# The last expert's output is rounded earlier and subtracted later; one transposed output and a scaling of rows move, in a fused retention, mixture-of-experts and feed-forward kernel

## The chip, the cores and the metric

The kernel runs on one core of a Trainium2 chip. The metric is the time of one execution on the device in microseconds (us): the median of the runs. The profile comes from one execution of its own, whose span runs from its first to its last instruction.

## The reference

Three stages follow one another on 1536 tokens of 512 features. A retention layer of 8 heads makes the rows x. A mixture of 8 experts sends each row to the expert with the largest logit, and scales that expert's output by the row's gate weight. A feed-forward stage with 2048 hidden features applies a rational function between its two matrix products.

```python
state = gamma * state + einsum('bhd,bhe->bhde', k_t, v_t)
y_t = scale * einsum('bhd,bhde->bhe', q_t, state)
...
expert_idx = argmax(x @ w_gate, axis=1)          # 8 experts, at most capacity rows each
h = maximum(einsum('ecd,edf->ecf', disp, w1), 0) # 512 -> 1024
y = einsum('ecf,efd->ecd', h, w2)                # 1024 -> 512
out[i] = gate_w[i] * y[expert_idx[i], pos[i]]
...
h = x @ w_in                                     # 512 -> 2048
P = a[0] + a[1]*h + a[2]*h*h + a[3]*h*h*h
Q = 1 + |b[0]|*|h| + |b[1]|*h*h
return (P / (Q + 1e-6)) @ w_out                  # 2048 -> 512
```

## The kernel before

Each fp32 factor of a product is split in two: a high part (`yh`, `xh`, `whi`, `gh`), rounded to the type fp32r by ScalarE, and a low part (`yl`, `xl`, `wlo`, `gl`), the difference, made by VectorE or GpSimd. A product is three matmuls: high by high, low by high, high by low.

Every engine works through its instructions in the order in which the Python code issues them; nothing reorders them. A semaphore makes an instruction wait for what it needs from another engine, and everything behind it on its own engine waits too.

**Experts.** `moe` loops over experts 1 to 7 (expert 0 is done in `first_expert`). The first layer of an expert has four blocks, `fp` 0 to 3, of 24 matmuls of 224 columns each. Behind each block stand a ReLU on ScalarE (`h`), the low part on VectorE, the split of another half of a weight block (`prep_next`: `whi` on ScalarE, `wlo` on VectorE) and a slot for decoding weights of the feed-forward stage (`dec_slot`, tile `gq`). The second layer has four quarters, `q` 0 to 3, of eight pairs of matmuls, which add up in `acc`: two tiles of two PSUM banks each. Behind the last quarter `y_pair` rounds each tile to `yh` (L856) and subtracts to `yl` (L857, L859). Both go to columns that start at a register's value, which a TENSOR_LOAD reads on both engines (`start`).

**The rows of the next experts.** Rows of expert `e` are fetched by an indirect DMA on GpSimd's queue (`gather`, two pieces for each expert, four buffers `xg`), scaled by their gate weight on ScalarE (`x_gate`, L954, in place), transposed by TensorE into a PSUM bank (`expert_x`, L964) and split into `xh` and `xl` (L967, L968). The tag `xt` of this bank has one buffer, which is bank 0; `y_turn` uses it too, for the transposed output `ytp` of the rest of expert 0 (`y0`, 96 rows), which it then splits (L850, L856, L857).

**Feed-forward.** `ffn_step(n)` issues block n of 48: `ffn_a` (first layer, 12 matmuls of 512 columns into one of the four banks with the tag `fh`, which `ffn_e` of block n-4 must have read), `ffn_i`, `ffn_p`, `ffn_r` and `ffn_e` (the rational function, on ScalarE, VectorE and GpSimd), `ffn_g` (high and low part `gg`) and, five blocks behind, `ffn_b` (second layer, 12 matmuls into the four banks with the tag `fo`). Steps 0 to 3 are issued between the quarters of expert 7, step 4 behind the first tile's `y_pair`. Blocks 0 to 7 read rows 0 to 1023 of `yh` and `yl`, while the last expert writes at row 1312 or behind it. The banks of the tag `fo` are those of the two `acc` tiles: the pool `pf` is opened when `pn` has been closed.

```python
"fh": (0, 1, 2, 3), "fo": (4, 5, 6, 7)      # banks; "xt": (0,)
...
self.pn = self.pool("pn", space=PSUM, stack=st)   # acc, in moe
...
self.pf = self.pool("pf", space=PSUM, stack=st)   # fo, in ffn
```

Of the kernel before, what the change touches and what calls it, by code (L numbers as in the profile page):

```python
# [7 lines left out]
F32 = mybir.dt.float32  # L8
# [5 lines left out]
AF = mybir.ActivationFunctionType  # L14
ALU = mybir.AluOpType
# [6 lines left out]
E = 8  # L22
# [18 lines left out]
NA = 48  # L41
# [43 lines left out]
class Build:  # L85
# [766 lines left out]

    def y_put(self, ps, k, at, more=None):
        yh, yl = self.yh[:, k, at], self.yl[:, k, at]
        tt = self.nc.vector.tensor_tensor
        self.nc.scalar.activation(out=yh, in_=ps, func=AF.Copy)  # L856
        tt(out=yl if more is None else yl.bitcast(F32), in0=ps, in1=yh.bitcast(F32), op=ALU.subtract)  # L857
        if more is not None:
            tt(out=yl, in0=more, in1=yl.bitcast(F32), op=ALU.add)  # L859

# [111 lines left out]
    def moe(self):  # L972
        nc = self.nc
        with ExitStack() as st:
# [8 lines left out]
            for e in range(1, E):  # L983
                xh, xl = (t.pop(e)[:, :, 0:W] for t in (self.xh, self.xl))
                h = {}
                for fp in range(4):
                    i = 4 * e + fp // 2
# [15 lines left out]
                    self.prep_next()  # L1003
                    if fp < 3 and fp != 1 and e + 1 < E:
                        self.x_gate(e + 1, fp // 2)
                    if fp % 2 and e + 1 < E:
# [4 lines left out]
                    if (e, fp) == (1, 0):  # L1011
                        self.y_turn(self.y0, 1)
                acc = [self.wide(i, "acc").rearrange("p (o n) -> p o n", o=2)[:, :, 0 : 2 * W] for i in range(2)]
                acc = [t.rearrange("p o (a n) -> p o a n", a=2) for t in acc]
                for q in range(4):
# [14 lines left out]
                    if q == 3:  # L1030
                        at = bass.ds(self.start(e), W)
                        for i in range(2 if e < E - 1 else 0):
                            self.y_pair(acc, i, at)
                    self.dec_slot(8 * e + 4 + q)
                    if e == E - 1:
                        self.ffn_step(q)
                    if q % 2:
                        del self.whi[4 * e + 2 + q // 2], self.wlo[4 * e + 2 + q // 2]
            for i in range(2):
                self.y_pair(acc, i, at)  # L1040
                if i == 0:
                    self.ffn_step(4)

    def y_pair(self, acc, i, at):
        self.y_put(acc[i][:, :, 0], slice(2 * i, 2 * i + 2), at, acc[i][:, :, 1])

# [181 lines left out]
    def ffn(self):  # L1228
        with ExitStack() as st:
            self.fp = self.pool("ffn", stack=st)  # L1230
            self.pf = self.pool("pf", space=PSUM, stack=st)
            for n in range(5, NA):
                self.ffn_step(n)
            self.ffn_tail()
# [179 lines left out]
```

## Time and profile before

| | before |
|---|---|
| time, median of 3 runs | 514.39 us (513.76 to 514.82) |
| the profiled execution's own time | 512.93 us |
| its span | 511.2 us |
| TensorE busy | 496.5 us |
| VectorE busy | 413.9 us |
| ScalarE busy | 365.4 us |
| GpSimd busy | 243.5 us |

The profiled execution's own time is 1.73 us above its span, and the median of the runs lies another 1.46 us above that. In the profile PE is TensorE's matmuls, DVE is VectorE, ACT is ScalarE and POOL is GpSimd; a small q behind an engine's name is its sequencer. L and a number is a line of the kernel.

### The profile page before, as it was taken

Reading aid. Unit: us, or ns where it says so; the run is one execution under the profiler, and the core shown is the slowest. Engines: PE = TensorE matmul, PEld = TensorE weight load, DVE = VectorE, ACT = ScalarE, POOL = GpSimd, SP = SyncE. Lnnn points to the kernel's source line nnn. Section 1 sums busy time; section 2 is a strip of 40 time slices with the busy share of each in tenths; the row PEclk is TensorE's granted clock in tenths of the full one; section 3 lists DMA queues with packets and bytes.
Section 4 is the critical chain, followed back from the end, with each engine's and each line's share of the span. In section 5 each row is a group of like instructions: output and inputs, shape, how many; then the busy total and the mean of one; then the engine's idle time right before and its main releaser. Section 6 shows DMA issues by size and latency. Waiting matters only on the chain.

```text
span 511.2 us, 9195 instructions
## 1 busy us (share of the span) xinstructions
PE 496.5 (97%) x3401; PEld 430.9 (84%) x3401; DVE 413.9 (81%) x602; ACT 365.4 (71%) x605; POOL 243.5 (48%) x187
## 2 busy tenths in 40 slices
PE   8999999999999999999879999999999999999995
PEld 5888878999999999998668888888888888888883
DVE  2579858789997999894686989999899998865973
ACT  1356638868767677664857989989999987776760
POOL 2621041034243744543424547667568764354774
PEclk9999999999999999999989999999999999999999
DMA  8999676899987999971400002222013100000203
GB/s 304 408 414 388 215 226 205 325 324 297 320 298 225 382 306 269 322 243 30 164 0 2 0 4 79 83 82 83 27 58 113 52 1 0 2 1 0 83 21 144
DMA packets 27409, 83.07 MB, mean 163 GB/s; under 512 B 4960, under 2 KB 5216, under 8 KB 27360
## 3 DMA queue, kind: packets, MB, share of 16 engines
q1 hardware_dynamic: 24304, 73.52, 42.2%
q0 software_dynamic: 2624, 7.35, 4.1%
q10 hardware_dynamic: 432, 1.57, 1.0%
q8 instruction: 27, 0.44, 0.3%
q14 instruction: 22, 0.18, 0.1%
HBM read 71.94 MB, written 10.49 MB: 161 GB/s over the span
## 4 chain that ended last, share of the span: by engine, by line
PE 62%; DVE 3%; ACT 2%; POOL 1%; issue 1%; POOLq 0%; ACTq 0%; DVEq 0%
PE h L1116 8%; PE h L1117 8%; PE h L1118 8%; PE o L1187 8%; PE o L1188 8%; PE o L1189 8%; PE acc L373 7%; PE e L996 2%; PE e L995 2%; PE e L994 2%; POOL out L1218 1%; PE tp L964 1%; DVE fw L1153 1%; DVE h L1154 1%; ACT fx L1129 0%
## 5 line engine op out<-in xcount | busy, mean ns | idle before, releaser
L154 DVE TENSOR_TENSOR wlo<-raw,whi 128x1024 fp32r<-128x1024 f32 x80 | 112.5, 1418 | 12.8 <-ACT whi L149 12.3
L1167 POOL TENSOR_TENSOR gg<-fx,gg 128x512 fp32r<-128x512 f32 x47 | 61.0, 1299 | 76.1 <-issue 60.8
L149 ACT ACTIVATE whi<-raw 128x1024 fp32r<-128x1024 f32 x80 | 83.2, 1056 | 2.0 <-PE acc L373 1.3
L1187 PE MATMUL o<-whi,gg 128*128 128x512 f32 x192 | 75.5, 393 | 4.6 <-DVE yl L859 4.6
L1188 PE MATMUL o<-wlo,gg 128*128 128x512 f32 x192 | 75.2, 392 | 0.0
L1189 PE MATMUL o<-whi,gg 128*128 128x512 f32 x192 | 75.2, 392 | 0.0
L1116 PE MATMUL h<-yh,whi 128*128 128x512 f32 x192 | 74.8, 390 | 0.0
L1118 PE MATMUL h<-yh,wlo 128*128 128x512 f32 x192 | 74.8, 389 | 0.0
L1117 PE MATMUL h<-yl,whi 128*128 128x512 f32 x192 | 74.7, 389 | 0.0
L373 PE MATMUL acc<-h,whi 128*128 128x448 f32 x224 | 71.3, 377 | 0.0
L1142 POOL TENSOR_TENSOR fw<-fh,fw 128x512 f32<-128x512 f32 x48 | 64.2, 1338 | 12.8 <-ACT fw L1131 12.0
L1129 ACT ACTIVATE fx<-h,ct 128x512 f32<-128x512 f32 x48 | 37.3, 777 | 42.9 <-PE h L1118 41.2
L209 POOL TENSOR_TENSOR gq<-gq 128x512 int32<-128x512 int32 x16 | 26.9, 1684 | 85.0 <-DVE gq L206 38.7
L994 PE MATMUL e<-xh,whi 128*128 128x224 f32 x224 | 62.1, 277 | 0.1
L996 PE MATMUL e<-xh,wlo 128*128 128x224 f32 x224 | 61.5, 274 | 0.0
L995 PE MATMUL e<-xl,whi 128*128 128x224 f32 x224 | 61.5, 274 | 0.0
L373 PE MATMUL acc<-h,wlo 128*128 128x224 f32 x224 | 59.0, 263 | 0.0
L1187 PEld LDWEIGHTS o<-whi,gg 128*128 128x128 f32 x192 | 36.4, 190 | 13.0 <-ACT fh L1130 5.0
L373 PEld LDWEIGHTS acc<-h,whi 128*128 128x128 f32 x224 | 42.0, 187 | 3.2
L994 PEld LDWEIGHTS e<-xh,whi 128*128 128x128 f32 x224 | 43.0, 192 | 0.5 <-ACT yh L856 0.4
L1153 DVE SCALAR_TENSOR_TENSOR fw<-fw,cq,h 128x512 f32<-128x512 f32 x48 | 35.6, 741 | 9.7 <-ACT h L1148 9.7
L995 PEld LDWEIGHTS e<-xl,whi 128*128 128x128 f32 x224 | 43.0, 192 | 0.0
(167 smaller groups left out, 1111.3 us busy)
## 6 DMA issues: line engine op xcount, KB each, us to landing
raw<-wm SPq DMA_DIRECT2D x61, 512.0 KB
r<-wf SPq DMA_DIRECT2D x32, 512.0 KB
kv<-kv SPq DMA_DIRECT2D x22, 512.0 KB
wd<-gq SPq DMA_DIRECT2D x16, 256.0 KB
raw<-wd SPq DMA_DIRECT2D x8, 512.0 KB
xd<-xs SPq DMA_DIRECT2D x12, 256.0 KB
raw<-wm ACTq DMA_DIRECT2D x3, 512.0 KB
kv<-kv SPq DMA_DIRECT2D x3, 256.0 KB
```

The source lines that it names most:

```text
L149: nc.scalar.activation(out=self.whi[i][:, sl], in_=raw, func=AF.Copy)
L154: (eng or self.nc.vector).tensor_tensor(out=self.wlo[i][:, sl], in0=raw, in1=self.whi[i][:, sl].bitcast(F32), op=ALU.subtract)
L373: self.nc.tensor.matmul(out, lhsT=w, rhs=x, start=start, stop=stop, skip_group_check=True)
L994: nc.tensor.matmul(ps[:, fi], lhsT=wh[:, sl], rhs=xh[:, k], start=(k == 0), stop=False)
L995: nc.tensor.matmul(ps[:, fi], lhsT=wh[:, sl], rhs=xl[:, k], start=False, stop=False)
L996: nc.tensor.matmul(ps[:, fi], lhsT=wl[:, sl], rhs=xh[:, k], start=False, stop=(k == 3))
L1116: nc.tensor.matmul(h, lhsT=wh[:, sl], rhs=self.yh[:, k, ts], start=(k == 0), stop=False)
L1117: nc.tensor.matmul(h, lhsT=wh[:, sl], rhs=self.yl[:, k, ts], start=False, stop=False)
L1118: nc.tensor.matmul(h, lhsT=wl[:, sl], rhs=self.yh[:, k, ts], start=False, stop=(k == 3))
L1187: self.nc.tensor.matmul(ps, lhsT=gh[:, ms], rhs=wh[:, ws], start=first, stop=False)
L1188: self.nc.tensor.matmul(ps, lhsT=gh[:, ms], rhs=wl[:, ws], start=False, stop=False)
L1189: self.nc.tensor.matmul(ps, lhsT=gl[:, ms], rhs=wh[:, ws], start=False, stop=last)
```

## The change

The last expert's two roundings, L856, are issued in front of `ffn_step(3)`, and all four of its subtractions behind that step and ahead of step 4. Step 4 is issued once the pools have changed. `y_put` is cut in two for this (`y_high`, `y_low`); for the other experts the order of the four instructions on each engine stays as it was. `y_turn(y0)` moves from behind the first block of expert 1's first layer to behind the first quarter of its second layer. `x_gate` of a first piece moves: from block 0 of the expert ahead to the third quarter of the expert ahead of that one (expert 2's stays where it was).

```diff
-    def y_put(self, ps, k, at, more=None):
+    def y_put(self, ps, k, at):
         yh, yl = self.yh[:, k, at], self.yl[:, k, at]
-        tt = self.nc.vector.tensor_tensor
         self.nc.scalar.activation(out=yh, in_=ps, func=AF.Copy)
-        tt(out=yl if more is None else yl.bitcast(F32), in0=ps, in1=yh.bitcast(F32), op=ALU.subtract)
-        if more is not None:
-            tt(out=yl, in0=more, in1=yl.bitcast(F32), op=ALU.add)
+        self.nc.vector.tensor_tensor(out=yl, in0=ps, in1=yh.bitcast(F32), op=ALU.subtract)
+
+    def y_high(self, acc, k, at):
+        self.nc.scalar.activation(out=self.yh[:, k, at], in_=acc[:, :, 0], func=AF.Copy)
+
+    def y_low(self, acc, k, at):
+        yh, yl, tt = self.yh[:, k, at], self.yl[:, k, at], self.nc.vector.tensor_tensor
+        tt(out=yl.bitcast(F32), in0=acc[:, :, 0], in1=yh.bitcast(F32), op=ALU.subtract)
+        tt(out=yl, in0=acc[:, :, 1], in1=yl.bitcast(F32), op=ALU.add)
...
                     self.prep_next()
-                    if fp < 3 and fp != 1 and e + 1 < E:
-                        self.x_gate(e + 1, fp // 2)
+                    if fp == 2 and e + 1 < E:
+                        self.x_gate(e + 1, 1)
...
                     if (e, fp) == (1, 0):
-                        self.y_turn(self.y0, 1)
+                        self.x_gate(2, 0)
...
                     if q == 3:
                         at = bass.ds(self.start(e), W)
-                        for i in range(2 if e < E - 1 else 0):
-                            self.y_pair(acc, i, at)
+                        y = [(acc[i], slice(2 * i, 2 * i + 2), at) for i in range(2)]
+                        for t in y:
+                            self.y_high(*t)
+                            if e < E - 1:
+                                self.y_low(*t)
+                    if (e, q) == (1, 0):
+                        self.y_turn(self.y0, 1)
+                    if q == 2 and e + 2 < E:
+                        self.x_gate(e + 2, 0)
                     self.dec_slot(8 * e + 4 + q)
                     if e == E - 1:
                         self.ffn_step(q)
...
-            for i in range(2):
-                self.y_pair(acc, i, at)
-                if i == 0:
-                    self.ffn_step(4)
+            for t in y:
+                self.y_low(*t)
...
-            for n in range(5, NA):
+            for n in range(4, NA):
                 self.ffn_step(n)
```

**ScalarE around `ffn_step(3)`.** The rows begin with the last instruction of step 2 (`h`, a reciprocal); `gg` is the rounding of block 0 and then of block 1, the three rows with `h_3456` or `h_3458` and what follows from them are block 3's, and ISA sets the column at which `yh` starts. Before:

```order
L1148 ACTIVATE h_3361<-fh_3336 128x512
L863 TENSOR_LOAD st8_83
L1165 ACTIVATE gg_3469<-fx_3334 128x512
L1129 ACTIVATE fx_3419<-h_3456,ct_61 128x512
L1130 ACTIVATE fh_3421<-h_3456 128x512
L1131 ACTIVATE fw_3420<-fh_3421,b0a_67,b1a_68 128x512
L1147 ACTIVATE fh_3421<-fw_3420,cq_66 128x512
L1148 ACTIVATE h_3403<-fh_3421 128x512
L856 ISA
L856 ACTIVATE yh_1129<-acc_3296 128x2x224
L1165 ACTIVATE gg_3499<-fx_3334 128x512
```

And now:

```order
L1155 ACTIVATE h_3361<-fh_3336 128x512
L868 TENSOR_LOAD st8_83
L859 ISA
L859 ACTIVATE yh_1129<-acc_3296 128x2x224
L859 ISA
L859 ACTIVATE yh_1129<-acc_3297 128x2x224
L1172 ACTIVATE gg_3471<-fx_3334 128x512
L1136 ACTIVATE fx_3419<-h_3458,ct_61 128x512
L1137 ACTIVATE fh_3421<-h_3458 128x512
L1138 ACTIVATE fw_3420<-fh_3421,b0a_67,b1a_68 128x512
L1154 ACTIVATE fh_3421<-fw_3420,cq_66 128x512
L1155 ACTIVATE h_3403<-fh_3421 128x512
```

Both roundings now stand ahead of block 0's `gg`; before, the first stood behind five activations on blocks 3 and 2 (and the second behind those on blocks 4 and 3).

**VectorE at the same place.** `yl` are the subtractions; `fx`, `fw` and `h` are the rational function, the last row of a block being the `fx` that `gg` then rounds. The rows begin with that of block 1. Before:

```order
L1155 SCALAR_TENSOR_TENSOR fx_3334<-fw_3335,h_3361 128x512
L857 ISA
L857 TENSOR_TENSOR yl_1130<-acc_3296,yh_1129 128x2x224
L859 ISA
L859 TENSOR_TENSOR yl_1130<-acc_3296,yl_1130 128x2x224
L1140 TENSOR_TENSOR fx_3419<-fx_3419,h_3456 128x512
L1141 SCALAR_TENSOR_TENSOR fx_3419<-fx_3419,ct_61,h_3456 128x512
L1153 SCALAR_TENSOR_TENSOR fw_3420<-fw_3420,cq_66,h_3403 128x512
L1154 SCALAR_TENSOR_TENSOR h_3403<-fx_3419,ct_61,h_3403 128x512
L1155 SCALAR_TENSOR_TENSOR fx_3419<-fw_3420,h_3403 128x512
L857 ISA
L857 TENSOR_TENSOR yl_1130<-acc_3297,yh_1129 128x2x224
```

And now:

```order
L1162 SCALAR_TENSOR_TENSOR fx_3334<-fw_3335,h_3361 128x512
L863 ISA
L863 TENSOR_TENSOR yl_1130<-acc_3296,yh_1129 128x2x224
L864 ISA
L864 TENSOR_TENSOR yl_1130<-acc_3296,yl_1130 128x2x224
L863 ISA
L863 TENSOR_TENSOR yl_1130<-acc_3297,yh_1129 128x2x224
L864 ISA
L864 TENSOR_TENSOR yl_1130<-acc_3297,yl_1130 128x2x224
L1147 TENSOR_TENSOR fx_3419<-fx_3419,h_3458 128x512
L1148 SCALAR_TENSOR_TENSOR fx_3419<-fx_3419,ct_61,h_3458 128x512
L1160 SCALAR_TENSOR_TENSOR fw_3420<-fw_3420,cq_66,h_3403 128x512
```

The second tile's subtractions moved ahead of the five instructions on blocks 3 and 2 that stood between the two tiles.

**TensorE in expert 1.** `ytp` is the transposed output of `y_turn(y0)`, `e1` are the accumulators of a first layer, `acc` those of the second. Before, it stood between blocks 0 and 1 of the first layer:

```order
L994 MATMUL e1_1328<-xh_1243,whi_1256 128x224
L995 MATMUL e1_1328<-xl_1244,whi_1256 128x224
L996 MATMUL e1_1328<-xh_1243,wlo_1257 128x224
L850 MATMUL ytp_1367<-ct_61,y_1316 128x96 x4
L994 MATMUL e1_1378<-xh_1243,whi_1256 128x224
L995 MATMUL e1_1378<-xl_1244,whi_1256 128x224
L996 MATMUL e1_1378<-xh_1243,wlo_1257 128x224
```

Now it stands between quarters 0 and 1 of the second layer, and so behind expert 2's second transposition (`tp`), which uses the same bank:

```order
L373 MATMUL acc_1497<-h_1353,whi_1320 128x448
L373 MATMUL acc_1497<-h_1353,wlo_1321 128x224
L850 MATMUL ytp_1520<-ct_61,y_1316 128x96 x4
L373 MATMUL acc_1496<-h_1392,whi_1320 128x448
L373 MATMUL acc_1496<-h_1392,wlo_1321 128x224
```

The four transpositions moved past the three other blocks of the first layer, two transpositions of expert 2's rows and eight pairs of the second layer.

## Rows read from the trace of the kernel before

**Rows 1.** The page, part 1: busy us of TensorE (share of the span), instructions.

```profile
PE 496.5 (97%) x3401; PEld 430.9 (84%) x3401; DVE 413.9 (81%) x602; ACT 365.4 (71%) x605; POOL 243.5 (48%) x187
```

**Rows 2.** Waits of TensorE: waiting, released by, total us, times, longest.

```profile
PE o L1187 <- DVE yl L859: 4.6, 1, 4.6
...
PE tp L964 <- ACT xg L954: 0.8, 1, 0.8
...
PE tp L964 <- DVE yl L857: 0.6, 1, 0.6
```

**Rows 3.** Stretches: length, busy PE, PEld, DVE, ACT, POOL, clock, DMA share, GB/s.

```profile
258.20:261.20 3.00, 3.00 (x7) 2.41 (x8) 2.93 (x5) 1.89 (x4) 2.25 (x2) 0.52 0.00 0
261.20:300.00 38.80, 38.80 (x173) 32.10 (x172) 29.15 (x41) 28.92 (x45) 15.60 (x13) 1.00 0.00 1
300.00:400.00 100.00, 100.00 (x443) 82.81 (x442) 94.38 (x132) 94.60 (x151) 68.14 (x50) 1.00 0.23 74
```

**Rows 4.** Timeline of TensorE, feed-forward: start, length, line, form [idle, releaser].

```profile
253.25 0.39 PE L1118 MATMUL h<-yh,wlo 128*128 128x512 f32 x1
258.20 0.77 PE L1187 MATMUL o<-whi,gg 128*128 128x512 f32 x1 [4.56 <-DVE yl L859]
...
261.22 0.40 PE L1188 MATMUL o<-wlo,gg 128*128 128x512 f32 x1
...
262.36 0.39 PE L1116 MATMUL h<-yh,whi 128*128 128x512 f32 x1
```

**Rows 5.** Timeline of ScalarE there.

```profile
245.68 0.60 ACT L1148 ACTIVATE h<-fh 128x512 f32<-128x512 f32 x1
247.76 0.64 ACT L1165 ACTIVATE gg<-fx 128x512 fp32r<-128x512 f32 x1 [1.49 <-DVE fx L1155]
...
251.59 0.53 ACT L856 ACTIVATE yh<-acc 128x448 f32 x1
```

**Rows 6.** Timeline of VectorE there.

```profile
252.15 0.62 DVE L857 TENSOR_TENSOR yl<-acc,yh 128x448 f32 x1 [2.38 <-ACT yh L856]
...
253.35 0.68 DVE L1140 TENSOR_TENSOR fx<-fx,h 128x512 f32<-128x512 f32 x1
...
254.73 0.74 DVE L1153 SCALAR_TENSOR_TENSOR fw<-fw,cq,h 128x512 f32<-128x512 f32 x1
...
256.17 0.69 DVE L1155 SCALAR_TENSOR_TENSOR fx<-fw,h 128x512 f32<-128x512 f32 x1
```

**Rows 7.** Timeline of TensorE, expert 1.

```profile
86.61 0.50 PE L850 MATMUL ytp<-ct,y 96*128 96x96 f32 x4
...
87.08 0.27 PE L995 MATMUL e<-xl,whi 128*128 128x224 f32 x1
...
90.42 0.66 PE L964 MATMUL tp<-ct,xg 128*128 128x128 f32 x4 [0.61 <-DVE yl L857]
...
99.21 0.37 PE L373 MATMUL acc<-h,whi 128*128 128x448 f32 x1
```

**Rows 8.** Timeline of ScalarE, expert 1.

```profile
93.78 0.55 ACT L999 ACTIVATE h<-e 128x448 fp32r<-128x448 f32 x1 [1.96 <-PE e L996]
```

**Rows 9.** Timeline of VectorE, experts 1 and 4.

```profile
99.58 0.55 DVE L968 TENSOR_TENSOR xl<-tp,xh 128x384 fp32r<-128x384 f32 x1
...
160.82 0.68 DVE L968 TENSOR_TENSOR xl<-tp,xh 128x512 fp32r<-128x512 f32 x1
```

**Rows 10.** Timeline of TensorE, expert 4.

```profile
156.63 0.66 PE L964 MATMUL tp<-ct,xg 128*128 128x128 f32 x4 [0.77 <-ACT xg L954]
...
162.49 0.60 PE L964 MATMUL tp<-ct,xg 128*128 128x128 f32 x4
```

**Rows 11.** Timeline of GpSimd, a gather in expert 4.

```profile
159.96 1.82 POOL L914 DMA_INDIRECT xg<-xd,gidx  x1
```

**Rows 12.** DMA from 159.9 to 169.5 us: GpSimd's queue, packets, MB, share.

```profile
q0 software_dynamic: 155, 0.52, 13.8%
```

**Rows 13.** Timeline of ScalarE, expert 4.

```profile
169.69 2.00 ACT L149 ACTIVATE whi<-raw 128x1024 fp32r<-128x1024 f32 x2
```

More of the change, by code (lines that the diff above doesn't have):

```diff
@@ L1038, in moe @@
                         del self.whi[4 * e + 2 + q // 2], self.wlo[4 * e + 2 + q // 2]
-            for i in range(2):
-                self.y_pair(acc, i, at)
-                if i == 0:
-                    self.ffn_step(4)
-    def y_pair(self, acc, i, at):
-        self.y_put(acc[i][:, :, 0], slice(2 * i, 2 * i + 2), at, acc[i][:, :, 1])
+            for t in y:
+                self.y_low(*t)
     def overflow(self):
```

## The prediction

> **What bounds the kernel now.** I read first how busy the engines are: TensorE works for 496.5 us of a span of 511.2, 97% [rows 1]. So the time can only fall where TensorE stands still or runs slowly, or where it is given less work. The change gives it the same matmuls in almost the same order, so next I read whom TensorE waits for [rows 2]. Besides some waits in the attention stage, which the change does not touch, the list has three: 4.6 us in the feed-forward stage for `yl`, 0.8 us for a scaled `xg`, and 0.6 us for the `yl` of a transposed output. Each has an edit in the diff. Behind the long wait TensorE also runs at half its clock: from 258.2 to 261.2 us the granted clock is 0.52 of full speed, most of it at the lower of its two levels, 1.2 GHz, and 1.00 behind it [rows 3]. It had stood idle since the last `h` matmul.
>
> **The large term: the last expert's output.** Full-speed matmuls of 512 columns follow one another 0.228 us apart: from 261.22 to 262.36 there are five [rows 4]. The last `h` matmul of block 5 starts at 253.25, so the first `o` was due at 253.48; it started at 258.20. That is 4.72 us of waiting (the profile's 4.56 counts from the end of the last matmul, not from when the next could start). The twelve `o` matmuls of block 0 then took 262.36 - 258.20 = 4.16 us instead of 12 x 0.228 = 2.74, which is another 1.42 us at the slow clock. Together 6.14 us.
>
> Why it waited: the `o` banks are the `acc` banks, and the second tile's last subtraction ended just ahead of 258.20. VectorE had itself stood idle for 2.38 us until 252.15 for the first rounding [rows 6], which ScalarE reached at 251.59, behind block 3's work [rows 5]. What it rounds was complete long before: the last `acc` matmul stands 36 `h` matmuls (blocks 3 to 5) ahead of 253.48, so at about 253.48 - 36 x 0.228 = 245.3.
>
> What takes its place: the two roundings now stand behind the `h` that starts at 245.68 and ahead of the `gg` at 247.76. ScalarE was idle there for 1.49 us, waiting for VectorE [rows 5]. Two roundings of 0.53 us, 1.06 us together, fit: I cost them at nothing. If they did not fit, they would delay `gg` by at most 1.06 us, and block 0's `gg` is not needed before 253.48. VectorE is free at 252.15 - 2.38 = 249.77. One tile's pair of subtractions takes 253.35 - 252.15 = 1.20 us [rows 6], so four end at about 252.17, 1.3 us before the `o` matmuls are due. The wait goes, and with it the slow clock, since TensorE no longer stands idle.
>
> What is late next: after block 0's `o` TensorE is due at 253.48 + 2.74 = 256.22 with block 6's `h`, which needs block 2's bank, so the end of `ffn_e(2)`. On VectorE the part of block 3 takes 254.73 - 253.35 = 1.38 us and `ffn_e(2)` takes 256.17 + 0.69 - 254.73 = 2.13 [rows 6]. So it ends at 252.17 + 1.38 + 2.13 = 255.68, 0.54 us early. I take 6.14 us in full. The bounds: none is lost, or the subtractions start no earlier than before, at 252.15, and `ffn_e(2)` ends at 258.06, which leaves a wait of 1.84 us.
>
> **The scaling of rows.** `x_gate` takes the same time wherever it stands; only one of its old places was waited for. In expert 4 the transposition at 156.63 waited 0.77 us for it [rows 10]; measured from when it could have started, as above (0.16 us more), 0.93. `x_gate` for expert 5 now stands in expert 3, ahead of the branch on overflow and of expert 4's first ReLU. What else holds that stretch? The next transposition, at 162.49 before, would be due at 161.56. It needs the bank that VectorE's `xl` frees at 160.82 + 0.68 = 161.50 [rows 9], and nothing moved is ahead of that `xl`. It just fits: 0.93 us gained; bounds 0 and 0.93.
>
> The moved scalings now stand in ScalarE's queue ahead of a split of weights and the roundings of the expert before, so ScalarE must never come to rows not yet fetched. The tightest is expert 6's first piece: its gather is issued at 159.96 [rows 11]; by 169.5 the 0.52 MB of this gather and the next have all moved [rows 12]; ScalarE comes to it behind the first of the two splits that start at 169.69 [rows 13], so at about 170.7. Cost nothing. Without that cover, what is delayed is a split of weights and two roundings that nothing of TensorE needs for several us.
>
> **The transposed output in expert 1.** At its old place it cost TensorE 87.08 - 86.61 - 0.11 = 0.36 us (0.11 is the usual spacing of 224 columns), and through the bank that it shares it held the next transposition for 0.61 us, 0.77 from when that could have started [rows 7]. So without it everything up to quarter 1 comes 1.13 us earlier: quarter 1, at 99.21 before, would be due at 98.08. But it now stands right there, behind expert 2's second transposition in the same bank, and must wait for VectorE's `xl` of that. This ended at 99.58 + 0.55 = 100.13 [rows 9]. ScalarE's last idle time ahead of it is before the ReLU at 93.78, where it waits for TensorE [rows 8]; so the chain from there to `xl` moves with TensorE, to 99.00. With 0.06 us for the signal `ytp` starts at 99.06 instead of 98.08, a new wait of 0.98 us, and quarter 1 starts at 99.06 + 0.36 = 99.42. This edit loses 0.21 us. The bounds: no wait at all, a gain of 0.77; or the `xl` no earlier than before, `ytp` at 100.19, a loss of 1.34.
>
> **The sum.** 6.14 + 0.93 - 0.21 = 6.86 us, about 6.9. Behind each place TensorE is the engine that the others wait for, so I let it pass to the end. The profiled execution took 512.93 us, its span 511.2: I expect 504.3 for the span and 506.1 for that execution. The runs' median stands 1.46 us above it, 514.39; so 507.5 for the runs.
>
> **The rivals.**
> A new wait in place of the old. If the roundings run as late as before, or VectorE's row of work slips past its 0.54 us to spare, block 6's `h` waits for its bank, by up to 1.84 us: 507.5 + 1.8 = 509.4. For it: the margin is small. Against: the 1.49 us of idle ScalarE.
>
> Given back later. From 300 to 400 us ScalarE is busy for 94.60 and VectorE for 94.38 of 100 us [rows 3]. The pause gave both a lead over TensorE. If they were the bound there, TensorE would wait later for what it saved: all of it back is 514.4, half 511. Against: TensorE shows no wait there, and from 261.2 to 300 VectorE works for only 29.15 of 38.80 us and ScalarE for 28.92 [rows 3], so 9.7 us are there to make up a lead of 6.1.
>
> Slower. The transposed output waits in the middle of expert 1's second layer, and each us for which expert 2's `xl` is late is a us of TensorE, with nothing behind to cover it. `xl` comes last of a row on ScalarE and VectorE in which, between two ReLUs, a decoding of transferred weights stands; a late transfer would hold all of it. The change ends slower than before by over 0.2% once that wait reaches 0.98 + 6.86 + 1.03 = 8.9 us, so with `xl` later than about 107; at 10 us it is 507.5 + 9.0 = 516.5, and the slow clock adds its 1.4 (a pause of 4.7 us brought it on above). Against: before, the `xl` ended at 100.13, and nothing in its chain waited for a transfer. The Trainium skill, in "TensorE: Matmul & The Clock Gate", in the table of figures at its head, says that the queues of ScalarE and VectorE are strict first in, first out. By that rule the `xl` cannot overtake a held row, which is what this rival needs; the trace agrees as far as VectorE's 2.38 us of idleness ahead of a held subtraction, with work on block 3 right behind it [rows 6].
>
> Nothing happens. If the first `o` is held by something that the profile names wrongly, such as the change of pools itself, the time stays at 514, less what expert 4 gives.
>
> **How the numbers follow.** Forecast 0.75, a new wait 0.11, given back 0.07 (half of it still faster), nothing 0.04, slower 0.03. A change within 0.2%, about 1.03 us, is about what a measurement of this kernel can tell from none. Faster: 0.75 + 0.11 + 0.05 = 0.91; same 0.06; slower 0.03. The likeliest case's time is 507.5. Below it lies the bound on the transposed output, which without a wait gives 0.98 more: 506.5; above it the new wait's 509.4. The three runs lie up to 0.6 us from their median, so the range is 506.1 to 509.8.
>
> **What would show it.** Right: no wait of `o` for `yl` and no clock below 1.00 near 253 us; the two roundings between 246 and 248; four subtractions in a row from 249.8; no wait of `tp` for `xg` in expert 4; one new wait of about 0.8 us (by the profile's count) of `ytp` for `xl` near 99 us. Wrong: waits of `h` or `o` for VectorE between 256 and 300 us, more idle time of TensorE beyond 300 us, or ScalarE idle for a gathered `xg`.

## The result, and the profile after

The changed kernel takes 508.39 us, the median of four runs (507.40 to 508.96), beside 514.61 for the kernel before (four runs, 513.76 to 517.39): a fall of 6.2 us. The ratio of the mean times, which is the ratio given for every run below, is 0.9868, 95% interval 0.9827 to 0.9908. The profiled execution took 508.29 us, its span 506.5. So between the two profiled executions the span fell by 4.7 us, where the sum had 6.86: most of the gain came, and about 2.2 us of it went somewhere. (By the medians less is missing, 0.6 us: the execution that was profiled before lay 1.7 us under the median of the runs, the one after lies at it.)

The page's part 1 for the changed kernel, busy us as in [rows 1]:

```profile
PE 494.5 (98%) x3401; PEld 429.6 (85%) x3401; DVE 412.8 (82%) x602; ACT 365.3 (72%) x605; POOL 243.8 (48%) x187
```

Its waits of TensorE, which answer to [rows 2]:

```profile
PE tp L969 <- DVE xl L973: 1.3, 1, 1.3
PE wp L302 <- DVE wu L647: 1.0, 1, 1.0
PE tp L533 <- DVE rr L527: 0.9, 1, 0.9
PE ytp L850 <- DVE xl L973: 0.8, 1, 0.8
```

All three waits of [rows 2] are gone. Two have come: `ytp`, which was forecast, and 1.3 us of a `tp` for `xl`, which was not. (The waits for `wu` and `rr` are in the attention stage, which was not edited; the one for `rr` was 0.3 us before.) Stretches of the feed-forward stage (FFN below), in the columns of [rows 3]:

```profile
253.00:255.00 2.00, 2.00 (x11) 1.65 (x10) 1.93 (x5) 1.97 (x5) 1.49 (x2) 1.00 0.00 0
255.00:257.71 2.71, 2.71 (x13) 2.25 (x12) 2.67 (x5) 2.68 (x5) 1.41 (x2) 1.00 0.00 0
300.00:400.00 100.00, 100.00 (x443) 82.81 (x442) 94.93 (x134) 94.72 (x152) 69.03 (x51) 1.00 0.23 74
```

The clock stays at its upper level, and block 0's twelve `o` matmuls pass in 2.71 us. Next the timeline of TensorE at the places of [rows 4, 7, 10], and in expert 6. (A `tp` "of expert 4" or "in expert 4" is one that TensorE does while it works on expert 4; it transposes rows of expert 5.)

```profile
98.53 0.26 PE L373 MATMUL acc<-h,wlo 128*128 128x224 f32 x1
99.61 0.55 PE L850 MATMUL ytp<-ct,y 96*128 96x96 f32 x4 [0.81 <-DVE xl L973]
...
156.52 0.60 PE L969 MATMUL tp<-ct,xg 128*128 128x128 f32 x4
...
162.52 0.63 PE L969 MATMUL tp<-ct,xg 128*128 128x128 f32 x4
...
205.67 0.27 PE L1001 MATMUL e<-xh,wlo 128*128 128x224 f32 x1
207.21 0.63 PE L969 MATMUL tp<-ct,xg 128*128 128x128 f32 x4 [1.27 <-DVE xl L973]
...
254.77 0.39 PE L1125 MATMUL h<-yh,wlo 128*128 128x512 f32 x1
255.00 0.39 PE L1194 MATMUL o<-whi,gg 128*128 128x512 f32 x1
...
257.71 0.39 PE L1123 MATMUL h<-yh,whi 128*128 128x512 f32 x1
```

TensorE executes nearly the same matmuls in both kernels, so the start of one instruction in the two traces, subtracted, gives a shift, and each step of the shift is a gain or a loss at that place:

| instruction | before | after | shift | step |
|---|---|---|---|---|
| a `tp` behind attention, ahead of all edits | 67.12 | 67.72 | +0.60 | +0.60, nothing edited there |
| expert 2's first `tp` | 112.09 | 112.90 | +0.81 | +0.21, the turn |
| expert 4's first `tp` | 156.63 | 156.52 | -0.11 | -0.92, the scaling |
| expert 4's second `tp` | 162.49 | 162.52 | +0.03 | +0.14, new |
| expert 6's second `tp` | 205.72 | 207.21 | +1.49 | +1.46, new |
| the first `o` | 258.20 | 255.00 | -3.20 | -4.69, the long wait |
| block 6's `h` | 262.36 | 257.71 | -4.65 | -1.45, the slow clock |
| a late `o` | 477.24 | 472.59 | -4.65 | 0 |

Every term of the forecast's sum has its size to within 0.05 us in this pair of traces. What is missing is in three rows that the sum had not: +0.60 ahead of all edits, +0.14 in expert 4 and +1.46 in expert 6.

ScalarE, in the feed-forward stage and on the way to expert 6:

```profile
155.35 0.54 ACT L1004 ACTIVATE h<-e 128x448 fp32r<-128x448 f32 x1 [2.71 <-SPq L1062]
...
170.03 0.67 ACT L197 ACTIVATE gq<-r 128x512 f32<-128x512 f32 x1 [3.32 <-DMA wd<-gq]
...
195.32 0.67 ACT L197 ACTIVATE gq<-r 128x512 f32<-128x512 f32 x1 [3.30 <-DMA wd<-gq]
...
247.75 0.96 ACT L859 ACTIVATE yh<-acc 128x448 f32 x2
249.30 0.63 ACT L1172 ACTIVATE gg<-fx 128x512 fp32r<-128x512 f32 x1 [0.59 <-DVE fx L1162]
```

The two roundings stand at 247.75 in a row, and `gg` behind them waits for VectorE as before, only 0.59 us in place of 1.49 [rows 5]. VectorE:

```profile
99.00 0.55 DVE L973 TENSOR_TENSOR xl<-tp,xh 128x384 fp32r<-128x384 f32 x1
...
206.39 0.68 DVE L973 TENSOR_TENSOR xl<-tp,xh 128x512 fp32r<-128x512 f32 x1
...
251.23 0.62 DVE L863 TENSOR_TENSOR yl<-acc,yh 128x448 f32 x1
...
253.07 0.62 DVE L864 TENSOR_TENSOR yl<-acc,yl 128x448 f32 x1
...
256.43 0.69 DVE L1162 SCALAR_TENSOR_TENSOR fx<-fw,h 128x512 f32<-128x512 f32 x1
```

The four subtractions end at 253.69, 1.31 us ahead of the first `o`, and `ffn_e(2)` at 257.12, 0.59 us ahead of block 6's `h`. The bank that expert 6's second `tp` needs comes free only with the `xl` at 206.39. Before, that `xl` stood at 203.22 and ended 1.8 us ahead of the `tp`:

```profile
203.22 0.67 DVE L968 TENSOR_TENSOR xl<-tp,xh 128x512 fp32r<-128x512 f32 x1
205.72 0.60 PE L964 MATMUL tp<-ct,xg 128*128 128x128 f32 x4
```

So it is 3.17 us later, with TensorE only 0.06 us later on the way there.

What made it late can be followed back. ScalarE's decoding at 195.32 waits for the store of an earlier decoded piece to land, since it writes into that piece's buffer (at 192.13 before, after 1.42 us). That store was issued at about the same time (184.58 against 184.92), but landed late, 10.6 us behind its issue. The rows of before:

```profile
176.82 2.12 SPq L162 DMA_DIRECT2D raw<-wm  x2
184.92 0.33 SPq L233 DMA_DIRECT2D wd<-gq  x1
192.13 0.67 ACT L197 ACTIVATE gq<-r 128x512 f32<-128x512 f32 x1 [1.42 <-DMA wd<-gq]
```

The queue of SyncE (SPq), which issues the loads of weights (`raw`) and the stores (`wd`), shows where DMA fell behind. Now:

```profile
175.02 0.38 SPq L162 DMA_DIRECT2D raw<-wm  x1
176.85 0.33 SPq L233 DMA_DIRECT2D wd<-gq  x1
177.27 5.19 SPq L162 DMA_DIRECT2D raw<-wm  x2
...
184.58 0.33 SPq L233 DMA_DIRECT2D wd<-gq  x1
```

Two loads of weights take 5.19 us to issue (2.12 before), in a stretch in which the DMA engines move 131, 35 and 88 GB/s (176 to 182 us in steps of 2; 342, 188 and 172 before). GpSimd's queue carries the scatters of the permutation there, words of 4 bytes. Those, the earlier wait at 170.03 and TensorE's own lead were the suspects.

### The profile page after: what moved, and what is told of

Read it like the earlier page. It is cut to its first block, busy times and chain, and to the rows that moved or that the text cites. A ratio compares the mean times of both kernels' runs of the same rounds, so it can differ in the third digit from the quotient of the medians.

```text
span 506.5 us, 9194 instructions
## 1 busy us (share of the span) xinstructions
PE 494.5 (98%) x3401; PEld 429.6 (85%) x3401; DVE 412.8 (82%) x602; ACT 365.3 (72%) x605; POOL 243.8 (48%) x187
## 4 chain that ended last, share of the span: by engine, by line
PE 61%; DVE 2%; DMA 2%; issue 2%; POOL 1%; ACT 1%; POOLq 0%; DVEq 0%; ACTq 0%
PE h L1125 9%; PE h L1123 9%; PE h L1124 9%; PE o L1196 8%; PE o L1194 8%; PE o L1195 8%; PE acc L373 6%; DMA wd<-gq 2%; PE e L999 2%; PE e L1001 2%; PE e L1000 2%; POOL out L1225 1%; DVE wlo L154 1%; PE tp L969 0%; ACT whi L149 0%
## 5 line engine op out<-in xcount | busy, mean ns | idle before, releaser
L1001 PEld LDWEIGHTS e<-xh,wlo 128*128 128x128 f32 x224 | 43.0, 192 | 0.0
L373 PEld LDWEIGHTS acc<-h,wlo 128*128 128x128 f32 x224 | 42.7, 191 | 0.1
```

The lines of the kernel that those rows point to most:

```text
L373: self.nc.tensor.matmul(out, lhsT=w, rhs=x, start=start, stop=stop, skip_group_check=True)
L1001: nc.tensor.matmul(ps[:, fi], lhsT=wl[:, sl], rhs=xh[:, k], start=False, stop=(k == 3))
```

## Experiments

Theories for what took back 1.4 us in expert 6: **the scatters** of single words slow the DMA engines, so that stores land late; **the moved scalings** delay ScalarE's pieces; **the lead**, that TensorE was let ahead of a chain which the change doesn't bring forward. For the large term there is the rival that the wait only moves on.

**The FFN part alone** (the kernel before, with the rounding split off):

```diff
-                        for i in range(2 if e < E - 1 else 0):
-                            self.y_pair(acc, i, at)
+                        for t in y:
+                            self.y_high(*t)
+                            if e < E - 1:
+                                self.y_low(*t)
...
-            for n in range(5, NA):
+            for n in range(4, NA):
```

> The kernel before with the rounding and subtracting of expert 7's output split (roundings ahead of block 3, block 4 and subtractions behind it), nothing else moved. The forecast's sum: the span 6.1 us shorter, all of it between expert 7 and the second transformed block of the FFN, TensorE's distance to the kernel before constant from there to the end; no new wait in experts 1 to 6. A rival theory, that the early roundings only shift the wait to a later block, expects 4.3 us or less.

Measured: 507.51 us (six runs, 506.21 to 508.72) against 513.74, ratio 0.9868 (0.9839 to 0.9897). The span of the profiled execution is 504.4. The first `o` starts at 252.93, without a wait:

```profile
252.93 0.39 PE L1190 MATMUL o<-whi,gg 128*128 128x512 f32 x1
```

Its shift to the kernel before is -0.55 us ahead of the FFN and -6.71 behind it to the end: 6.16 gained, as forecast, and the rival's 4.3 or less did not come. No wait in expert 6. (The 0.55 ahead of it comes from the wait for `xg` in expert 4: 0.15 us in this execution and 0.77 in the other, with nothing changed there.)

**The scaling alone:**

```diff
-                    if fp < 3 and fp != 1 and e + 1 < E:
+                    if (fp == 2 or (e, fp) == (1, 0)) and e + 1 < E:
...
+                    if q == 2 and e + 2 < E:
+                        self.x_gate(e + 2, 0)
```

> The kernel before with only the first scaling of rows of experts 3 to 7 moved to the third quarter two experts ahead; expert 2's scaling and the turn of expert 0's outputs stay. Forecast: TensorE gains 0.93 us in expert 4 and keeps it: the span 0.9 us shorter. If the moved scaling itself delays ScalarE's next pieces (the theory that it causes the new wait of expert 6's second transpose for VectorE), the wait of about 1.3 us stands at that transpose here too and the span is 0.3 to 0.6 us longer. If slow landings of decoded weights behind the scatters of single words cause it, the wait comes or not by how late those stores land in this execution: none if ScalarE's decode in expert 5 waits under 2 us.

Measured: 514.74 us (twelve runs), ratio 1.0011 (0.9991 to 1.0030): no change. The profiled execution is the slowest of the twelve, 517.08 us. The timeline of TensorE, in expert 6 and at the first `o`:

```profile
208.55 0.63 PE L964 MATMUL tp<-ct,xg 128*128 128x128 f32 x4 [1.48 <-DVE xl L968]
...
261.04 0.77 PE L1189 MATMUL o<-whi,gg 128*128 128x512 f32 x1 [4.57 <-DVE yl L859]
```

The shift goes from +0.90 to -0.04 at expert 4's first `tp` (0.94 gained), then up to +0.62 (0.66 lost in experts 4 and 5), and from there to +2.83 in expert 6 (2.21 lost). So the move brings its 0.9 us at the first place, and the wait in expert 6 doesn't need the rest of the change. Which theory holds this run can't say: ScalarE's decoding in expert 5 waits 2.91 us for a store here too.

**The turn alone:**

```diff
-                    if (e, fp) == (1, 0):
-                        self.y_turn(self.y0, 1)
...
+                    if (e, q) == (1, 0):
+                        self.y_turn(self.y0, 1)
```

> The kernel before with only the second turn of expert 0's outputs moved behind the first quarter of expert 1's second product. Forecast: 1.13 us less of a wait at the old place, a new wait of 0.98 us at the new one and the rest of the loss: TensorE 0.2 us later behind expert 1 and to the end; the span the same within 0.3 us. No new wait in experts 5 and 6.

Measured: 514.91 us (twelve runs), ratio 1.0013 (0.9992 to 1.0035). The shift goes from +0.32 behind attention to +0.53 behind expert 1: 0.21 lost, as forecast. No wait in expert 6.

**The changed kernel again,** unedited:

> The changed kernel once more, nothing edited: a second trace of it. If the new wait of expert 6's second transpose (1.3 us) belongs to the order of instructions, it stands here again at the same place and size within 0.2 us, and TensorE's lateness of 0.6 us in attention too. If it comes from how late the decoded weights' stores land, its size differs by 0.5 us or more and follows the wait of ScalarE's decode in expert 5 (3.3 us in the first trace, 1.4 before); the span then moves with it. The total is 5 to 7 us under the kernel before.

Measured: 507.52 us (six runs, 506.48 to 508.33), ratio 0.9865 (0.9837 to 0.9892), span 506.6. The wait in expert 6 is there again, 1.08 us, and ScalarE's decoding in expert 5 waits 3.69 us. TensorE's lateness behind attention is 0.35 us in place of 0.60; over the traces it lies between 0.04 and 0.9 in kernels with the same code there. So that row of the table is scatter; the other came twice. The full change and its FFN part alone take the same time (507.52 and 507.51).

**The scatters moved** out of experts 4 to 7 into the FFN:

```diff
-                    if e >= 4 and q < 3:
-                        self.perm_put(3 * (e - 4) + q)
-                    if (e, q) == (7, 3):
-                        self.perm_get()
...
+        if 8 <= n < 20:
+            self.perm_put(n - 8)
+        if n == 22:
+            self.perm_get()
```

> The changed kernel with the twelve scatters of the permutation, and the load of the result, moved from experts 4 to 7 into blocks 8 to 22 of the FFN; nothing else. If the scatters of single words choke the DMA engines and that makes the new wait in expert 6, large packets no longer take over 2 us near 176 us, no stretch of 2 us between 176 and 182 falls under 100 GB/s, and expert 6's second transpose waits less than 0.3 us: the span is 1.4 us shorter than the changed kernel's. If the wait comes from TensorE having been let ahead of the chain of decoding (expert 4's gain only lent), it stands there with at least 0.7 us.

Measured: 507.12 us (four runs, 506.23 to 509.10), ratio 0.9868 (0.9835 to 0.9901); span 504.7, with no wait in expert 6. The DMA view from 174 to 182 us, first of the changed kernel (KB of each issue, median us to landing):

```profile
raw<-wm SPq DMA_DIRECT2D x3, 512.0 KB, 11.0
wd<-gq SPq DMA_DIRECT2D x1, 256.0 KB, 10.4
pd<-ids,row POOLq DMA_INDIRECT x1, 8.4
```

and with the scatters moved:

```profile
raw<-wm SPq DMA_DIRECT2D x3, 512.0 KB, 7.0
wd<-gq SPq DMA_DIRECT2D x1, 256.0 KB, 5.8
```

A store lands after 5.8 us in place of 10.4. (It is the one ahead of the store that the late decoding waits for.) TensorE's shift still rises by 0.17 us at expert 6's second `tp`, at 205.37, since the `xl` ends only 0.14 us ahead of it:

```profile
204.55 0.68 DVE L973 TENSOR_TENSOR xl<-tp,xh 128x512 fp32r<-128x512 f32 x1
```

So without the scatters the wait is gone, but not the time to spare, 1.8 us in the kernel before. The span came out 1.8 us shorter than in the first trace of the changed kernel, where 1.4 was expected and 0.5 of it is attention's scatter. The total times of the two kernels can't be told apart.

**The scalings at their old place** in the changed kernel (all but expert 2's):

```diff
-                    if fp == 2 and e + 1 < E:
-                        self.x_gate(e + 1, 1)
+                    if (fp == 2 or fp == 0 and e > 1) and e + 1 < E:
+                        self.x_gate(e + 1, fp // 2)
...
-                    if q == 2 and e + 2 < E:
-                        self.x_gate(e + 2, 0)
```

> The changed kernel with the first scaling of experts 3 to 7 back at its old place, so the change without its gain in expert 4. Expert 4's first transpose waits 0.15 to 1.4 us for the scaled rows again (four traces without the move differ by that). If the moved scaling is behind the wait in expert 6, that is gone, and the time equals the changed kernel's within 0.7 us: what the move gains in expert 4 it loses in expert 6. If the wait has nothing to do with the move, it stands, and the span is 0.5 to 1 us longer.

Measured: 508.29 us (four runs), ratio 0.9872 (0.9847 to 0.9897), span 506.9. Expert 4's `tp` waits 0.96 us for `xg` again. Expert 6's still waits 0.49 us: neither gone nor what it was. So the move is not needed for a wait there, and neither of the two cases expected came as it was put.

**One scaling moved, the wrong one:**

```diff
+                    if (fp == 2 or fp == 0 and e > 1 and e != 3) and e + 1 < E:
+                        self.x_gate(e + 1, fp // 2)
...
-                    if q == 2 and e + 2 < E:
+                    if (e, q) == (2, 2):
```

> The changed kernel with the scaling moved for expert 4 alone; for experts 3, 5, 6 and 7 it is back at its old place. If the moved scalings in experts 4 and 5, which stand between two splits of weights, delay the chain to expert 6, the wait there goes and expert 4's 0.9 us is kept: the span about 1.3 us shorter than the changed kernel's. If it is TensorE's own lead over the decoding (its stores hang on the branch on overflow, which the move doesn't bring forward) that is taken back, the wait stays at 0.7 us or more, and the span is the changed kernel's.

This moves, against the intention, the scaling of expert 4's rows, which are transposed in expert 3, where nothing waited; TensorE's wait in expert 4 is for expert 5's rows. So it is a second trace of the old place: 508.21 us, ratio 0.9880 (0.9858 to 0.9903), 0.43 us of wait for `xg`, none in expert 6.

**One scaling moved, the right one** (as above with `e != 4` and `(3, 2)`):

> The changed kernel with the first scaling moved for expert 5 alone, the one that TensorE waited for; for experts 3, 4, 6 and 7 it is back at its old place (the earlier run that meant to do this moved expert 4's, which is used in expert 3). Expert 4's gain of about 0.9 us is there. If the scalings moved into experts 4 and 5 delay the chain of decoding, expert 6's wait is under 0.2 us and the span 1.3 us under the changed kernel's. If TensorE's lead over that chain and the holes in the DMA rate behind the scatters make it, the last piece of expert 6's rows on VectorE is 2 to 3 us later against TensorE than before, and the wait is 0.3 to 1.3 us.

Measured: 507.85 us (four runs), ratio 0.9874 (0.9849 to 0.9898). Expert 4's gain is there (from +0.99 to +0.06, 0.93), and the wait in expert 6 stands, 0.82 us. The scalings moved into experts 4 and 5 (of experts 6 and 7) don't make it: with those two at their old place it came all the same.

**The kernel before with the scatters moved** (the same edit as above):

> The kernel before with only the scatters moved into the FFN. No stretch of 2 us between 176 and 182 under 200 GB/s. TensorE waits in expert 4 for the scaled rows as before and not in expert 6; so the time is that of before within 0.5 us: the scatters cost the kernel before nothing, and only the changed kernel, which leads the decoding by 0.8 us, feels them.

Measured: 514.53 us (ten runs), ratio 1.0005 (0.9991 to 1.0018). The kernel before did not pay for its scatters: the `xl` in expert 6 ends 2.2 us ahead of the `tp` here, 1.8 with the scatters.

**The roundings late:**

```diff
                         for t in y:
-                            self.y_high(*t)
                             if e < E - 1:
+                                self.y_high(*t)
                                 self.y_low(*t)
...
+            for t in y:
+                self.y_high(*t)
             for t in y:
                 self.y_low(*t)
```

> The changed kernel with the two roundings of the last expert's output behind block 3's instructions on ScalarE, as before; block 4 still ahead of the subtractions. The first rival's bound on a chip: the first output matmul stays without a wait of over 0.5 us only if the roundings still come by about 250; by the rows of before they come at 251.6 and the subtractions end about 1.9 us later than in the changed kernel, so TensorE waits at the first output matmul or for block 6's bank, 1 to 2 us in all, and the span is 1 to 3.3 us longer (the more if the slow clock comes back).

Measured: 509.21 us (four runs, 508.32 to 510.94), ratio 0.9902 (0.9870 to 0.9934). TensorE, at the first `o` and at block 6's `h`:

```profile
253.57 0.39 PE L1127 MATMUL h<-yh,wlo 128*128 128x512 f32 x1
255.11 0.47 PE L1196 MATMUL o<-whi,gg 128*128 128x512 f32 x1 [1.15 <-DVE yl L864]
...
258.44 0.50 PE L1125 MATMUL h<-yh,whi 128*128 128x512 f32 x1 [0.33 <-DVE fx L1164]
```

The roundings stand at 251.92, and TensorE waits at both places that the first rival named. Against the changed kernel's trace its shift goes from -1.20 ahead of the FFN to +0.90 behind it: 2.1 us lost. (The span, 507.4, is only 0.9 us longer, because expert 6's wait is 0.33 us here.) A pause of 1.15 us did not bring the slow clock: the granted clock is 1.00 from 252 to 262.

So ScalarE's idle time near 247 us brings the last 2.1 us of the FFN's gain, not all of it. Against the kernel before, TensorE's shift goes from +0.30 to -3.75, so 4.05 us come with the first rounding no earlier than it was. What is gone here is the gap behind it: in the kernel before the second tile's rounding, behind the work on blocks 4 and 3, came 4.2 us after the first, which started at 251.59:

```profile
255.82 0.53 ACT L856 ACTIVATE yh<-acc 128x448 f32 x1
```

**The turn one quarter later:**

```diff
-                    if (e, q) == (1, 0):
+                    if (e, q) == (1, 1):
                         self.y_turn(self.y0, 1)
```

> The changed kernel with the second turn of expert 0's outputs behind the second quarter of expert 1's second product in place of the first. The turn no longer waits for VectorE (0.81 us by the profile's count, 0.98 by when it could start): TensorE 1.0 us earlier behind expert 1. Expert 6's wait stands here, 0.3 to 1.5 us, and may take part of it; the span 0.5 to 1 us under the changed kernel's.

Measured: 506.58 us (six runs, 505.15 to 508.72), ratio 0.9858 (0.9835 to 0.9881), span 504.2. The turn doesn't wait; behind expert 1 the shift is -0.48 with +0.33 from attention, so 0.81 gained where the change lost 0.21. In expert 4 part of it goes again (next run). In expert 6 nothing waits, though the expectation had 0.3 to 1.5 us there.

**Both, the later turn and the scatters moved:**

> The changed kernel with both edits: the turn behind the second quarter and the scatters in the FFN. No wait of the turn, and expert 6's second transpose waits under 0.5 us. Forecast span 503.7 us, 0.8 to 1 under that of the changed kernel with only the scatters moved (504.7), and the total 7.5 to 8 us under the kernel before.

Measured: 506.03 us (five runs, 505.30 to 507.06), ratio 0.9844 (0.9825 to 0.9863), span 504.3. That is 0.4 us under the changed kernel with only the scatters moved, where 0.8 to 1 was expected. Expert 6 doesn't wait: its `xl`, the second row, ends 2.2 us ahead of the `tp`. TensorE in expert 4, the second `tp`, and that `xl`:

```profile
161.68 0.63 PE L969 MATMUL tp<-ct,xg 128*128 128x128 f32 x4 [0.80 <-DVE xl L973]
...
202.02 0.68 DVE L973 TENSOR_TENSOR xl<-tp,xh 128x512 fp32r<-128x512 f32 x1
```

ScalarE behind the branch on overflow (a jump on a flag at the end of expert 3, which every engine passes), first in the kernel before:

```profile
154.48 0.55 ACT L999 ACTIVATE h<-e 128x448 fp32r<-128x448 f32 x1 [2.64 <-SPq L1055]
```

and now:

```profile
154.51 0.55 ACT L1004 ACTIVATE h<-e 128x448 fp32r<-128x448 f32 x1 [3.45 <-SPq L1058]
```

TensorE came to the branch 0.77 us earlier than in the kernel before. Yet ScalarE passes it at 154.51, where it passed at 154.48 before: SyncE releases it, and SyncE did not come earlier. ScalarE's `h`, then `xh` and VectorE's `xl`, hang from there, and TensorE waits for the `xl`. So the chain behind this branch doesn't follow TensorE's lead: of the 0.77 us that TensorE brings there and the 0.93 of the scaling, 0.80 is left behind the second `tp`. With the later turn alone ScalarE passes at 154.54, with TensorE 0.48 us earlier, and the `tp` waits 0.53. What holds SyncE there no run sets apart. By the spans these two are 2.2 to 2.4 us under the changed kernel; by the runs' intervals they are not separated from it.

All traces together (lowest DMA rate in a step of 2 us between 176 and 182; wait of expert 6's second `tp` by the profile's count, a dash where none is listed):

| kernel | scatters in the experts | expert 5's scaling moved | GB/s | wait, us |
|---|---|---|---|---|
| before | yes | no | 172 | - |
| FFN part alone | yes | no | 115 | - |
| turn alone | yes | no | 215 | - |
| scalings at the old place | yes | no | 145 | 0.49 |
| wrong scaling moved | yes | no | 154 | - |
| changed | yes | yes | 35 | 1.27 |
| changed again | yes | yes | 25 | 1.08 |
| scaling alone | yes | yes | 35 | 1.48 |
| right scaling moved | yes | yes | 59 | 0.82 |
| roundings late | yes | yes | 158 | 0.33 |
| turn later | yes | yes | 228 | - |
| before, scatters moved | no | no | 406 | - |
| changed, scatters moved | no | yes | 297 | - |
| both | no | yes | 355 | - |

Without the scatters the rate stays at 297 or more in that stretch and nothing waits, in three traces of three. (Just behind it, from 182 to 186 us, it falls to 129 and 143 in two of these three.) With them it goes down to between 25 and 228 in all eleven, and the wait came in five of six with the scaling moved and in one of five without. So in these traces the wait came only with the scatters, and more often with the moved scaling. The code alone doesn't fix its size: up to the last expert "roundings late" has the instructions of the changed kernel, and it waits 0.33 us where that waited 1.27 and 1.08.

The part of the move that can be read is a lead of 0.8 us: in the changed kernel's trace TensorE's shift falls by 0.92 in expert 4, while SyncE's issue of the next store keeps its +0.87 (160.71 against 159.84). That alone is less than the 1.8 us that expert 6's `tp` had to spare. And the lead, the shift of that issue less the shift of expert 4's second `tp`, is 0.8 us in all eight traces with the scaling moved, among them "turn later", which doesn't wait, and "both", with 2.2 us to spare. So the lead alone does not make the wait. Why the rate falls to 25 to 59 in some traces and only to 228 in another with the same scatters stays open, and with it the cause of the 1.46 us; it may be how the issue of a load falls between the scatters, but no run here sets that apart.

## Why the prediction was right, and where its sum was not

The time, 508.39 (507.52 the second time), lies 0.9 us or less from the 507.5 forecast and inside the range, and the likeliest case is the one that came. That it lies so near is in part luck. For the profiled execution the forecast was 506.1, and 508.29 came, 2.2 us more. The forecast for the runs added the 1.46 us by which their median had stood above the profiled execution; now that distance is 0.10, and so 1.36 of the 2.2 us dropped out. By its steps:

**The long wait and the slow clock: right.** 6.14 forecast, 6.14 in the table, 6.16 alone. Roundings and subtractions stand where it put them once TensorE's lateness of 1.5 us is added; the forecast margins of 1.3 and 0.54 us came out as 1.31 and 0.59. The second bound ("the subtractions start no earlier than before", 1.84 us) was near the 2.1 that the late roundings cost, and it shows what the forecast's account of the wait leaves out: by the late roundings most of the term, 4.05 us, came from the second rounding, at 255.82, and only the rest from the first, at 251.59. What the forecast could not see in one trace is that the slow-clock term isn't fixed: its 1.42 us is the least of four (last section).

**The scaling: size right (0.93; 0.92 and 0.94 measured), and "it just fits" nearly so.** At the next transposition 0.14 us is lost in this trace, and 0.03 to 0.42 in the others with the turn at the same place or unmoved. Expert 6's rows were fetched in time. But the wait removed is itself loose: where it stands, it measured 0.15 to 1.37 us.

**The turn: right.** 0.98 of new wait forecast, 0.97 measured (99.61 - 98.53 - 0.11), 0.21 net here and alone. In other traces with the turn at that place it costs up to 0.65 net, with waits of 0.81 to 1.26 by the profile's count.

**The step that failed** is the one behind the sum: "Behind each place TensorE is the engine that the others wait for, so I let it pass to the end". Behind expert 4 it isn't. Decodings, and the subtractions on VectorE behind them, wait there for stores that must land, and in expert 6 TensorE waits for them. The forecast did not look up that this chain had only 1.8 us to spare; it followed the chain for the next transposition alone. With the 1.46 us there, 0.14 in expert 4 and 0.60 of attention's scatter the sum of 6.86 becomes the 4.7 measured. Why the stores land so late that the 1.8 us are used up is not shown (end of the experiments).

**The rivals.** "A new wait in place of the old" did not come in the FFN. "Given back later" came in part, yet not where it looked: nothing beyond 300 us, 1.4 us in expert 6. "Slower" needed an `xl` held by a late transfer in expert 1. That `xl` ended at 99.55, which is the 99.00 forecast plus attention's 0.60 to within 0.05; but the very mechanism, a transfer that holds ScalarE's row, bit in experts 4 and 5. There the rule of the Trainium skill cited with it ("TensorE: Matmul & The Clock Gate", the table at its head: strict order on ScalarE and VectorE) holds in the trace: behind the decoding held for 3.30 us until 195.32 every later piece of VectorE, down to the `xl`, is 3.2 us later than before. (ScalarE, which had idle time ahead of it, is back at its shift of 0.06 from 200.19.) On the transfers the Trainium skill says in "DMA: Bandwidth & Descriptors", under back-pressure in remote DMA, that stalled writes stall the other queues of the same DMA engine; it speaks of copies between cores. The traces agree as far as that the whole DMA rate can be low beside one queue's small writes (35 against 297 GB/s); whether by stalled writes no run here shows.

## What to carry to other kernels

A wait removed from the bounding engine can be taken back by a chain that doesn't hang from it: before adding it to a sum, follow the next few instructions that depend on transfers or on a branch, and read how long ahead of time each came. A wait for an instruction that only stands late in its engine's queue, with its input long complete, as the roundings here, is the better find: it gave all of its time and asked nothing of a transfer. Compare the start of one instruction in two traces, place by place, when terms are smaller than the spread of the runs.

## What the runs showed of the hardware

A pause of the same length costs a different time at the slow clock. In the kernel before the first `o` waits 4.56 us and the slow clock costs 1.42 by the forecast's count; in the trace of the scaling alone it waits 4.57 us, and the granted clock stays at 0.50, TensorE's lower level, for longer (columns as in [rows 3]):

```profile
262.00:264.00 2.00, 2.00 (x6) 1.58 (x5) 1.97 (x4) 0.94 (x2) 2.00 (x2) 0.50 0.00 0
264.00:266.00 2.00, 2.00 (x6) 1.52 (x6) 1.97 (x4) 0.00 (x0) 0.33 (x1) 0.50 0.00 0
266.00:268.00 2.00, 2.00 (x9) 1.61 (x8) 1.72 (x3) 0.00 (x0) 0.00 (x0) 0.83 0.00 0
```

From the first `o` at 261.04 to the one at 307.30 TensorE takes 46.26 us there. Between the same two it takes 44.96 in the profiled execution of before (258.20 to 303.16) and 43.51 in the changed kernel's (255.00 to 298.51), which has neither pause nor slow clock. So the pause of 4.56 us cost 1.45 us more in one execution and 2.75 in the other; in the traces of the turn alone and of the kernel before with the scatters moved, with waits of 4.55 and 4.57 us, it cost 2.4 and 1.7. The kernel before was spread over 512.61 to 516.86 us in one set of 23 runs, the changed kernel over 506.48 to 508.33 in six; part of the difference may be this.

Three scatters of 128 single words, 4 bytes each, went with a fall of the whole DMA rate from about 400 to as little as 25 GB/s for two us, and in the changed kernel's trace with 5.19 us in which SyncE could issue only two loads. The three traces without them in that place show nothing under 129 GB/s from 174 to 186 us; with them the lowest rate was 25 to 59 in four traces of eleven and 115 or more in the others.
